# First batch of a fused attention and two-layer MoE kernel: softmax over rows of tokens straight from PSUM, wider key and value products, trees for phi, and a new order

## The chip, the cores and the metric

One core of one Trainium2 chip runs the kernel. The metric is the device time of one execution in microseconds (us), lower is better. Five engines work side by side: TensorE (PE, with its weight loads listed as PEld), VectorE (DVE), ScalarE (ACT), GpSimd (POOL), and SyncE (SP), which issues most DMAs.

## The reference, cut to what matters

Sizes: 4 batches, 8 heads, 576 tokens a batch, head dimension 64, 32 memory slots; model width 512, first hidden width 2048, then 4 experts of hidden width 1024. All is float32.

```
a    = softmax(phi, over the 32 slots)                  # per batch, head, token
k_m  = einsum('bhsm,bhsd->bhmd', a, k);  v_m = the same with v
attn = softmax(q @ k_m^T / 8, over the 32 slots)
x    = concat_heads(attn @ v_m)                         # 2304 x 512
h    = x @ w_in;  g = max(0.01 h, h);  x = g @ w_out    # first MoE layer
out  = sum over e of p_e * (relu(x @ w1[e]) @ w2[e])    # second layer
```

## The kernel before, in words

**The stages.** Attention of the four batches runs inside the first MoE layer; the second MoE layer follows. The first layer never forms `attn @ v_m`. For a chunk of 256 hidden features it multiplies `v_m` by `w_in` (`y_pair`, L984) and splits the result into a rounded high part and a low rest; the hidden product (`moe1_step`, L968) then multiplies that by the attention weights, which are split in the same way into `ah` and `al`: three products for each of two groups of heads, six matmuls of 128x288 for a half batch and a chunk of 128 features. ACT applies the leaky rectifier (L1023), ACT and DVE split again, and three times four matmuls (L1035 to L1037) multiply by a chunk of `w_out`. The first layer goes by units of features (6, 6 and 4 chunks of 128); in a unit come batch 0's first half of tokens with all chunks, its second half, then batch 1, and so on. So the first product of the layer needs batch 0's `ah` and `al` of the first half and the first `y`.

**One batch of attention** (`att_batch`, L540 to L741). 128 partitions hold 8 heads by 16 blocks, in 2 groups of 64 partitions. `phi` is loaded into `pl`, its maximum over 9 rows taken (`tree`, L552), finished over partitions by two PE transposes (L570, L576), subtracted (L578), and the exponential written to `a` (L581). For `k` and `v`, 72 products of a 64x32 piece of `a` with 64 columns accumulate over 9 rows (L617; each counts twice in the profile, as every float32 matmul here). The sum of `a` (L628, L633) gives the reciprocal `rz`, and ACT or DVE scales the products into `kv` (L641 to L655). Transposes give `kb` (L673 to L680) for the keys and `vt` for the values.

**Queries and scores before.** A batch in `TURNED` (batch 1 alone) transposes `q` with 20 PE transposes into `qT` (L586 to L601), copied out of PSUM by ACT; the others use one DVE transpose of 2304 elements in blocks of 32 (L603). Scores come out with the slots on partitions (L702), so for each half of the tokens DVE transposes them out of PSUM (L707, L713), takes the maximum (L720), subtracts (L722), ACT exponentiates (L725), DVE sums (L727), inverts (L729), multiplies (L733, or POOL), and transposes back (L736); `split` (L739) writes `ah` by ACT and `al` by DVE or POOL. Each half has its own such chain.

**Weights.** `w_in` and `w_out` are float64: `piece64` (L861) turns a 512 KB piece to float32 by two ACT passes (L877, L882), one of DVE (L888) and one of POOL (L887), and `w_out` is split as well. Raw pieces wait for three buffers and four places in `xx`.

**What sets the order.** `Plan` collects every operation with an engine, a cost, a due time and its dependences, and `issue` (L106) plays them as a list schedule in which the earliest due goes first. The order that comes out is each engine's program order, fixed before the run; the engines wait for each other by semaphores. `two=True` keeps a DVE operation from starting in the plan while POOL works, and the reverse. `SHIFTS` (L20) is a list of (first operation, count, us) added to due times by hand or search. `AFTER` (L748) says behind which step a later batch's loads enter the plan. `HOME` (L510) gives places: the queries of batches 0, 2 and 3 all lie in `A0`. While PE has nothing to do in the first 50 us the plan inserts idle matmuls (`idle`, L485).

## Time and profile before

| what | us |
|---|---|
| median of 3 runs (lowest, highest) | 1135.43 (1135.03, 1136.18) |
| the profiled execution, its own time | 1134.85 |
| its span, first to last instruction | 1133.0 |
| TensorE busy in the span | 1111.4 (98%) |
| first hidden product of the first layer (L968) starts | 33.11 |
| mean granted TensorE clock | 0.996 of full speed |

The span is counted from the first instruction; all times within the trace are from there. Between the span and the execution's own time lie 1.85 us that no instruction fills. In a row, "x" counts instructions, and a bracket at the end says how long the engine was idle before and what released it. A matmul's end is modelled, so consecutive matmuls overlap in the list; the distance between starts is what one costs.

### The profile page before, as it was taken

How to read it: one execution, taken by the hardware profiler on the slowest of the kernel's cores; microseconds unless marked ns; L12 is line 12 of the kernel's file. 1: busy time of each engine (PE TensorE's matmuls, PEld its weight loads, DVE VectorE, ACT ScalarE, POOL GpSimd, SP SyncE). 2: the span in 40 equal slices, each digit the busy share in tenths (PEclk: the TensorE clock that was granted, in tenths of full speed). 3: DMA queues.
4: the chain of work that ended last, by engine and by line, in shares of the span. 5: the costliest groups of instructions: out<-in, count | busy, mean ns of one | idle time of the engine just before them, and what ended most of it. 6: DMA issues, size and time to landing. Idle time of an engine off the chain costs nothing.

```text
span 1133.0 us, 18259 instructions
## 1 busy us (share of the span) xinstructions
PE 1111.4 (98%) x7478; PEld 1007.8 (89%) x7478; DVE 656.2 (58%) x1209; ACT 434.9 (38%) x889; POOL 98.9 (9%) x106
## 2 busy tenths in 40 slices
PE   4999999999999999999999999999999999999998
PEld 2788999999999998998998899889998889999887
DVE  6876645433437787677677653454576644454543
ACT  4854577633436444333334223222223223212220
POOL 3531035400000000000000000000000000000000
PEclk9999999999999999999999999999999999999999
DMA  9933024300002285554443744444344653344402
GB/s 358 313 113 120 2 76 132 113 1 2 20 1 103 87 317 192 204 205 188 156 165 133 223 161 156 167 167 157 130 139 168 171 212 138 127 154 167 168 19 56
DMA packets 54440, 160.86 MB, mean 142 GB/s; under 512 B 6484, under 2 KB 22868, under 8 KB 48212
## 3 DMA queue, kind: packets, MB, share of 16 engines
q1 hardware_dynamic: 49172, 100.19, 25.6%
q0 software_dynamic: 4608, 58.72, 14.7%
q8 instruction: 58, 0.95, 0.3%
q10 hardware_dynamic: 576, 0.79, 0.2%
q14 instruction: 26, 0.21, 0.1%
HBM read 125.60 MB, written 34.08 MB: 141 GB/s over the span
## 4 chain that ended last, share of the span: by engine, by line
PE 96%; DVE 1%; issue 1%; ACT 1%; DMA 0%; POOL 0%; POOLq 0%; DVEq 0%
PE psum L1144 31%; PE psum L1214 12%; PE psum L1213 12%; PE psum L1212 12%; PE psum L968 9%; PE psum L1035 6%; PE psum L1037 6%; PE psum L1036 6%; PE psum L984 2%; PE psum L617 1%; PE psum L702 1%; DVE exact L554 1%; DMA att<-in_phi_dram 0%; PE psum L487 0%; DVE att L603 0%
## 5 line engine op out<-in xcount | busy, mean ns | idle before, releaser
L1153 DVE TENSOR_TENSOR exact<-psum,exact 128x384 f32<-128x384 f32 x336 | 184.1, 556 | 271.8 <-PE psum L1144 267.8
L1160 ACT ACTIVATE rounded<-exact 128x384 fp32r<-128x384 f32 x192 | 100.9, 525 | 293.2 <-DVE exact L1153 291.4
L353 DVE TENSOR_TENSOR rounded<-exact,rounded 128x288 fp32r<-128x288 f32 (+3 forms) x221 | 120.6, 561 | 117.2 <-ACT rounded L350 116.5
L1214 PE MATMUL psum<-late,rounded 128*128 128x512 f32 x384 | 150.7, 392 | 0.0
L1213 PE MATMUL psum<-late,rounded 128*128 128x512 f32 x384 | 150.5, 392 | 0.0
L1212 PE MATMUL psum<-late,rounded 128*128 128x512 f32 x384 | 149.3, 389 | 0.0
L1144 PE MATMUL psum<-rounded 128*128 128x384 f32 x768 | 143.2, 335 | 0.0
L1144 PEld LDWEIGHTS psum<-rounded 128*128 128x128 f32 x768 | 134.7, 188 | 2.4 <-DVE exact L1153 0.3
L968 PE MATMUL psum<-rounded 128*128 128x288 f32 x768 | 122.6, 296 | 0.0
L350 ACT CAST rounded<-exact 128x288 fp32r<-128x288 f32 (+4 forms) x237 | 113.6, 500 | 14.6 <-DVE exact L836 4.4
L1035 PE MATMUL psum<-rounded 128*128 128x288 f32 x384 | 115.3, 300 | 0.0
L1036 PE MATMUL psum<-rounded 128*128 128x288 f32 x384 | 113.0, 294 | 0.7 <-DVE rounded L353 0.7
L1037 PE MATMUL psum<-rounded 128*128 128x288 f32 x384 | 112.9, 294 | 0.0
L968 PEld LDWEIGHTS psum<-rounded 128*128 128x128 f32 x768 | 108.1, 188 | 4.3 <-issue 3.9
L1144 PE MATMUL psum<-late,rounded 128*128 128x384 f32 x576 | 109.7, 336 | 0.0
L1164 DVE SCALAR_TENSOR_TENSOR rounded<-exact,rounded 128x384 fp32r<-128x384 f32 x192 | 98.9, 551 | 12.9 <-ACT rounded L1160 12.9
L1144 PEld LDWEIGHTS psum<-late,rounded 128*128 128x128 f32 x576 | 102.1, 188 | 3.8
L1175 ACT COPY exact<-psum 128x384 f32<-128x384 f32 x48 | 23.0, 480 | 196.8 <-PE psum L1144 196.8
L1023 ACT ACTIVATE exact<-psum 128x288 f32<-128x288 f32 x128 | 52.5, 410 | 119.9 <-PE psum L968 112.2
L1214 PEld LDWEIGHTS psum<-late,rounded 128*128 128x128 f32 x384 | 72.0, 188 | 15.1
L1213 PEld LDWEIGHTS psum<-late,rounded 128*128 128x128 f32 x384 | 72.0, 188 | 13.4
L1212 PEld LDWEIGHTS psum<-late,rounded 128*128 128x128 f32 x384 | 72.1, 188 | 13.2
(105 smaller groups left out, 1615.9 us busy)
## 6 DMA issues: line engine op xcount, KB each, us to landing
rounded<-kept POOLq DMA_DIRECT2D x22, 1792.0 KB, 7.7
exact<-in_moe_w_dram SPq DMA_DIRECT2D x64, 512.0 KB
kept<-rounded SPq DMA_DIRECT2D x10, 1792.0 KB
w<-kept POOLq DMA_DIRECT2D x10, 1792.0 KB, 7.8
kept<-w SPq DMA_DIRECT2D x6, 1792.0 KB
exact<-in_moe_w_in_dram SPq DMA_DIRECT2D x16, 512.0 KB
exact<-in_moe_w_out_dram SPq DMA_DIRECT2D x16, 512.0 KB
out_dram<-exact SPq DMA_DIRECT2D x60, 64.0 KB
```

Of the source, the lines that this page charges most:

```text
L350: nc.scalar.copy(out, in_) if e == "ACT" else engine(e).tensor_copy(out, in_)
L353: engine(e).tensor_tensor(out=out, in0=in0, in1=in1, op=ALU.subtract)
L968: nc.tensor.matmul(ps, lhsT=l, rhs=r, start=start and n == 0, stop=stop and n == len(seq) - 1)
L1035: nc.tensor.matmul(po, lhsT=w2l[:, ds_], rhs=th, start=first, stop=False)
L1036: nc.tensor.matmul(po, lhsT=w2h[:, ds_], rhs=tl, start=False, stop=False)
L1037: nc.tensor.matmul(po, lhsT=w2h[:, ds_], rhs=th, start=False, stop=last)
L1144: nc.tensor.matmul(ps[k][0:TB], lhsT=l, rhs=r, start=(i == 0), stop=(i == 5))
L1153: plan.op("DVE", dve2(TB), at[k], lambda: nc.vector.tensor_tensor(out=o, in0=ps[k][0:TB], in1=other, op=ALU.add), [ps[k], ok, from_], [key])
L1160: plan.op("ACT", act2(TB), at[k], lambda: nc.scalar.activation(out=th, in_=src, func=AF.Relu), [key, *h_from[hs[c, i]]], [keys[0]])
L1212: nc.tensor.matmul(po[0:DM], lhsT=tl, rhs=w2h[:, c], start=(p == 0 and c == 0), stop=False)
L1213: nc.tensor.matmul(po[0:DM], lhsT=th, rhs=w2l[:, c], start=False, stop=False)
L1214: nc.tensor.matmul(po[0:DM], lhsT=th, rhs=w2h[:, c], start=False, stop=(p == NP2 - 1 and c == 1))
```

## The change

For batch 0 alone: `phi`'s maximum and `a`'s sum become four DVE operations on halves (`tree`; for later batches also where DVE and not POOL takes it); the key and value products take two heads at a time, 64x64 pieces with 128 columns, of which the blocks off the diagonal are not used; the scaling by `rz` is four DVE operations for keys and four for values; `q` is transposed by PE (`TURNED` is now batch 0, so batch 1 goes the block way with L603). The scores come out with tokens on partitions, as 72 products of 64x64 by 32 columns in two parts (5 and 4 pairs of blocks of 64 tokens), so the softmax is done per part directly from PSUM, with no DVE transpose; the weights go to the place of `q`, 9 PE transposes turn them, and ACT and DVE write `ah` and `al` from PSUM, each part for both halves of the tokens. `q2` is loaded behind the `v` step together with `v1`. A number of costs and `two` flags change in the plan, and `SHIFTS` is a new list.

```
-SHIFTS = [(149, 1, 40.3), (286, 2, -1.2), (123, 1, 4.3), (232, 2, -1.2), (141, 8, 4.5), (4, 5, 25.2),
...
+SHIFTS = [(84, 27, 12.7), (94, 12, 5.9), (281, 8, 4.8), (683, 24, 24.5), (362, 33, 3.6), (85, 22, -17.5),
...
-    TURNED = (1,)
+    TURNED = (0,)
...
         def tree(fold, rows, e="DVE"):
-            if e == "DVE":
-                nc.vector.tensor_reduce(
-                    out=tops[:, 0:P].rearrange("p (h m) -> p h m", h=rows.shape[1]),
-                    in_=rows.rearrange("p h r m -> p h m r"), axis=AX.X, op=fold)
-                return
             h = rows.shape[1]
...
-            op("DVE", 1.35, due, lambda: tree(ALU.max, rows), ["pl"], ["aT1"])
+            op("DVE", 1.75, due, lambda: tree(ALU.max, rows), ["pl"], ["aT1"], two=True)
...
-                    for h in range(HG):
+                    for h in range(0, HG, 1 + wide):
                         for g in range(NGB):
...
+                            if wide:
+                                out_ = pkv[g * 512:g * 512 + 2 * D][h * M:(h + 2) * M].rearrange("p (h d) -> p h d", h=2)
+                                lhsT, rhs = a[gs, r, hs].rearrange("p h m -> p (h m)"), src[gs, 0, hs, r * D:(r + 1) * D]
...
+                    for h in range(HG):
+                        hs, at_d = slice(h * M, (h + 1) * M), h % 2 * D
+                        in_ = pkv[0:1024].rearrange("p (g n) -> p g n", g=NGB)[hs, :, at_d:at_d + D]
+                        nc.vector.tensor_tensor(out=kv[hs, :, lo], in0=in_, in1=rz[hs].unsqueeze(2).to_broadcast([M, NGB, D]),
+                                                op=ALU.mult)
+                op("DVE", 1.2, due, fn, [pkv, "rz0"], [f"kv{g}{nm}" for g in range(NGB) for nm in names])
...
+            for x in range(2):
+                rs, first, count = slice(x * D, (x + 1) * D), x * (LT + 1) // 2, (LT + 1 - x) // 2
+                n, groups = count * HG * M, slice(first * HG, (first + count) * HG)
...
+                    for j in range(count):
+                        for h in range(HG):
+                            for g in range(NGB):
+                                at_s = (j * HG + h) * M
+                                nc.tensor.matmul(
+                                    ps[at_s:at_s + M][g * D:(g + 1) * D], lhsT=qT[rs, j, h, g * D:(g + 1) * D],
+                                    rhs=kb[rs, g, h * M:(h + 1) * M], start=True, stop=True)
+                op("PE", 0.4 * count, due, fn, ["qT0", "qT1", "qT2", "kb"], [ps])
...
+                op("DVE", dve(n), due, lambda mx_=mx_, score=score: nc.vector.tensor_reduce(
+                    out=mx_, in_=score(), axis=AX.X, op=ALU.max), [ps], km)
+                op("DVE", dve(n), due, lambda mx_=mx_, raised=raised, full=full, score=score: nc.vector.tensor_tensor(
+                    out=raised[:, :, 0:M], in0=score(), in1=mx_.unsqueeze(2).to_broadcast(full), op=ALU.subtract),
...
+                op("ACT", act(n), due, lambda raised=raised: nc.scalar.activation(
+                    out=raised[:, :, 0:M], in_=raised[:, :, 0:M], func=AF.Exp, scale=scale), [], ka)
+                op("DVE", dve(n), due, lambda sm_=sm_, raised=raised: nc.vector.tensor_reduce(
+                    out=sm_, in_=raised, axis=AX.X, op=ALU.add), ka, ks)
+                op("DVE", 0.29, due, lambda sm_=sm_: nc.vector.reciprocal(sm_, sm_), [], ks)
+                op("DVE", dve(n), due, lambda e, sm_=sm_, raised=raised, full=full, weight=weight: engine(e).tensor_tensor(
...
+                   ka + ks, [f"e{x}"], room=[qn], also=("POOL", n * 2.03e-3), two=True)
+            for x, n, count, weight in parts:
+                pt = Banks(psum, 2 - x)
...
+                    for j in range(count):
+                        nc.tensor.transpose(pt[j * P:(j + 1) * P], weight[:, j * P:(j + 1) * P], ident)
+                op("PE", 0.12 * count + 0.1, due, fn, [f"e{x}", qn, "ident"], [pt])
+                for s in range(2):
...
+                    op("ACT", act(n // 2), due, lambda part=part, column=column: copy("ACT", part(ah), column()),
+                       [pt], [f"h{x}{s}"])
+                    op("DVE", dve(n // 2), due, lambda part=part, column=column: subtract(
+                        "DVE", part(al), column(), part(ah).bitcast(F32)), [pt, f"h{x}{s}"], [f"l{x}{s}"])
...
-        ("phi", 0): ["p1"], ("q", 0): ["q2"], ("v", 0): ["v1"],
+        ("phi", 0): ["p1"], ("v", 0): ["q2", "v1"],
```

In the chains of all later batches the subtraction (L722) and the multiplication (L733) get `two=True`, and the DVE shift in `piece64` (L888) is planned at 0.45 us where it was 0.42.

## Rows read from the trace of the kernel before

**Rows 1.** The page's head and busy lines: span, busy time and share of each engine.
```profile
span 1133.0 us, 18259 instructions
...
PE 1111.4 (98%) x7478; PEld 1007.8 (89%) x7478; DVE 656.2 (58%) x1209; ACT 434.9 (38%) x889; POOL 98.9 (9%) x106
```

**Rows 2.** TensorE by stretch: us, length, busy (count), granted clock, DMA share, GB/s.
```profile
33.10:40.00 6.90, 6.90 (x64) 1.00 0.93 331
40.00:45.00 5.00, 4.27 (x43) 1.00 0.88 334
45.00:50.00 5.00, 3.98 (x30) 1.00 0.74 220
50.00:100.00 50.00, 49.95 (x757) 1.00 0.52 170
```

**Rows 3.** Chain of waits, its longest pieces: start us, us, what.
```profile
4.91 2.09 DVE exact L554
...
22.00 3.67 issue
```

**Rows 4.** Engines by stretch: length; busy of PE, PEld, DVE, ACT, POOL; clock; DMA share, GB/s.
```profile
4.90:18.40 13.50, 7.97 (x172) 4.12 (x173) 10.99 (x12) 8.19 (x14) 3.97 (x3) 1.00 1.05 398
18.40:33.10 14.70, 9.62 (x248) 4.79 (x248) 11.34 (x16) 8.15 (x16) 6.35 (x5) 0.77 1.03 378
```

**Rows 5.** Timeline of the start, all engines: start us, us, engine, line, operation.
```profile
7.62 0.29 DVE L571 TENSOR_REDUCE att<-psum 128x2 f32<-128x128 f32 x1 [0.63 <-PE psum L570]
...
11.33 2.28 DVE L554 TENSOR_REDUCE exact<-att 128x128 f32<-128x1152 f32 x1 [1.23 <-ACT att L581]
...
11.84 1.67 PE L617 MATMUL psum<-exact,att 64*32 64x64 f32 x144
...
14.64 0.52 ACT L652 ACTIVATE exact<-psum,att 128x64 f32<-128x64 f32 x2 [0.46 <-DVE att L638]
...
15.68 2.56 DVE L603 STREAM_TRANSPOSE att<-att 128x2304 f32<-128x2304 f32 x1
...
18.18 0.38 DVE L888 TENSOR_SCALAR exact<-exact 128x512 uint32<-128x512 uint32 x1
...
18.39 1.98 PE L702 MATMUL psum<-att,exact 32*32 32x288 f32 x64 [1.49 <-DVE att L603]
...
23.10 0.68 ACT L725 ACTIVATE att<-att 128x576 f32<-128x576 f32 x1 [0.96 <-DVE att L722]
...
29.82 1.29 POOL L887 TENSOR_TENSOR w<-w,exact 128x512 uint32<-128x512 uint32 x1 [0.92 <-ACT exact L882]
29.88 1.85 DVE L722 TENSOR_TENSOR att<-att 128x576 f32<-128x576 f32 x1
...
31.66 0.68 DVE L353 TENSOR_TENSOR rounded<-psum,rounded 128x512 fp32r<-128x512 f32 x1
...
33.11 3.45 PE L968 MATMUL psum<-rounded 128*128 128x288 f32 x24
```

**Rows 6.** Timeline of TensorE, 39 to 70 us (batch 1).
```profile
42.68 1.51 PE L596 MATMUL psum<-att,exact 128*64 128x128 f32 x12
...
51.83 2.25 PE L617 MATMUL psum<-exact,att 64*32 64x128 f32 x144
...
56.81 0.67 PE L668 MATMUL psum<-att,exact 128*64 128x128 f32 x8
...
58.97 0.79 PE L702 MATMUL psum<-att,exact 64*32 64x160 f32 x32
```

**Rows 7.** Timeline of TensorE from 70 us (first hidden product of batch 1, then batch 2).
```profile
70.93 1.05 PE L968 MATMUL psum<-rounded 128*128 128x288 f32 x6
...
93.33 0.64 PE L673 MATMUL psum<-att,exact 128*32 128x128 f32 x16
...
95.27 1.24 PE L702 MATMUL psum<-att,exact 32*32 32x288 f32 x32
```

**Rows 8.** Timeline of VectorE, 59 to 82 us (batch 1's first y).
```profile
68.43 1.16 DVE L353 TENSOR_TENSOR rounded<-psum,rounded 128x1024 fp32r<-128x1024 f32 x1
```

More of the change, by code (lines that the diff above doesn't have):

```diff
@@ L499 @@
     qD = qT.rearrange("p a h n -> p (a h n)")[:, 0:HG * LT * D].rearrange("p (h c e t) -> p h c e t", h=HG, c=LT, e=2)
-    at = [tile_([NR, M + 1]) for i in range(2)]
+    both_at_ = tile_([2 * NR, M + 1])
+    at = [both_at_[:, i * NR:(i + 1) * NR] for i in range(2)]
     aT = [tile_([NGB, HB]), exact(NGB, HB)]
@@ L504 @@
     spare = exact(512)
-    small = {nm: [tile_([n]) for i in range(2)]
-             for nm, n in (("mx", NR), ("sm", NR), ("nmx", NGB), ("rz", NGB))}
+    small_ = {nm: tile_([2 * n]) for nm, n in (("mx", NR), ("sm", NR), ("nmx", NGB), ("rz", NGB))}
+    small = {nm: [t[:, 0:t.shape[1] // 2], t[:, t.shape[1] // 2:]] for nm, t in small_.items()}
     places = {"A": tile_([1, HG, S]), "X": xx.rearrange("p h (b s) -> p b h s", b=B)}
@@ L564, in att_batch @@
         if b == 0:
-            op("DVE", 1.35, due, lambda: tree(ALU.max, rows), ["pl"], ["aT1"])
+            op("DVE", 1.75, due, lambda: tree(ALU.max, rows), ["pl"], ["aT1"], two=True)
         else:
-            op("DVE", 1.35, due, lambda e: tree(ALU.max, rows, e), ["pl"], ["aT1"], also=("POOL", 3.0))
+            op("DVE", 1.75, due, lambda e: tree(ALU.max, rows, e), ["pl"], ["aT1"], also=("POOL", 3.0), two=True)
         mr = tops[:, 0:P]
@@ L628, in att_batch @@
                 if b == 0:
-                    op("DVE", 1.35, due, total, ["a"], ["aT1"])
+                    op("DVE", 1.75, due, total, ["a"], ["aT1"], two=True)
                 else:
-                    op("DVE", 1.35, due, lambda e, total=total: total(e=e), ["a"], ["aT1"], also=("POOL", 3.0))
+                    op("DVE", 1.75, due, lambda e, total=total: total(e=e), ["a"], ["aT1"], also=("POOL", 3.0), two=True)
                 pz = Banks(psum, 1)
@@ L640, in att_batch, with fn @@
             lo = "kv".index(sorted(names, key=lambda nm: HOME[nm][b])[0])
-            for g in range(NGB):
+            if b == 0:
+                def fn(pkv=pkv, lo=lo):
+                    for h in range(HG):
[4 more added lines that the diff above has]
+                op("DVE", 1.2, due, fn, [pkv, "rz0"], [f"kv{g}{nm}" for g in range(NGB) for nm in names])
+            for g in range(NGB if b else 0):
                 def fn(e, g=g, pkv=pkv, n=len(names), lo=lo):
@@ L723, in att_batch @@
                 out=at_r, in0=at_r, in1=mx.unsqueeze(2).to_broadcast(wide), op=ALU.subtract),
-               km, ka, also=("POOL", pool(S)))
+               km, ka, also=("POOL", pool(S)), two=True)
             op("ACT", act(S), due, lambda at_r=at_r: nc.scalar.activation(
@@ L734, in att_batch @@
                 out=at_r, in0=at_r, in1=sm.unsqueeze(2).to_broadcast(wide), op=ALU.mult),
-               ks, ka, also=eng[1])
+               ks, ka, also=eng[1], two=True)
             op("DVE", dve(S), due, lambda s=s, at_r=at_r: nc.vector.transpose(
@@ L887, in add @@
             engine(e).tensor_tensor(out=out, in0=fu, in1=low, op=ALU.add)
-        plan.op("DVE", 0.42, due, lambda: nc.vector.tensor_single_scalar(fu, fu, 3, op=ALU.logical_shift_left),
+        plan.op("DVE", 0.45, due, lambda: nc.vector.tensor_single_scalar(fu, fu, 3, op=ALU.logical_shift_left),
                 [], [fk], two=True)
```

40 lines of the change are left out of this document (31 added, 9 removed), and 10 rows, old and new, of the table SHIFTS.

## The prediction

> **What bounds the kernel now.** I read the page's head first: TensorE is busy 1111.4 of 1133.0 us [rows 1], so the end moves only if TensorE gets less to do, or starts its real work earlier, or loses less between. The stretches by engine show where it loses: from 50 us on it has no gap worth naming (49.95 of 50 us), while of the 16.9 us from 33.1 to 50 it is busy 6.90 + 4.27 + 3.98 = 15.15, so 1.75 us idle [rows 2]. Before 33.11 us no hidden product of the MoE layer runs; the first starts there [rows 5], and everything TensorE does earlier (batch 0's attention, the first `y`, idle matmuls) is in the shade of whoever makes that product wait. So the end is the start of that product, called S, plus the idle time behind S, plus TensorE's fixed work behind S. I write each part of the change as a shift of one of these three.
>
> Who sets S? In the chain of waits the start is phi's landing, a maximum of 2.09 us on VectorE and so on, and the stretch view has VectorE busy 10.99 of 13.5 us, then 11.34 of 14.7 us up to S; ACT stands at 8.19 and 8.15 [rows 3, 4]. Its idle time is hand-over time in a chain that is serial: product, maximum, subtraction, exponential, sum. VectorE is thus the engine to add up for S. The chain also has 3.67 us at 22.00 us in which TensorE waited for nothing that the profile shows ("issue") [rows 3], inside the value products, with the DMA share above 1 [rows 4].
>
> **The steps up to S.** The price of a VectorE pass comes from two rows: 0.29 us for 128 elements and 0.68 for 512, both out of PSUM [rows 5], so 1.02 ns an element more; 256 cost 0.42, 320 cost 0.49, 576 cost 0.75, 640 cost 0.81.
>
> *phi's trees.* Four operations of 512, 256, 128 and 128 elements: 0.68 + 0.42 + 0.29 + 0.29 = 1.68 us, in place of 2.09 [rows 3] and 2.28 [rows 5]. Both lie on the chain: the exponential ends 0.4 us earlier, at 10.9 (before, the sum started behind it at 11.33), the sum's tree at 12.6.
>
> *Key products.* Before, 144 instructions of 64 columns took 1.67 us; in batch 1 144 of 128 columns took 2.25 [rows 5, 6]. The change issues 72 of 128 columns. Half of 2.25 is the lower bound, 2.25 the upper one; I take 1.9, as the two rows show that most of the time is per instruction but 0.58 us came with the columns. They end near 13.4, beside the tree and the division that follows it, which ended 1.0 us behind the sum (13.61 to 14.64): so `rz` stands at 13.6 and sets the pace, and the products cost nothing; without that cover they cost at most 0.1.
> By the Trainium skill (TensorEngine Tiling (Array Packing), Available Configurations) pieces of 64x32 leave eight independent tiles and 64x64 only four, which speaks against the wide form; by it alone the products stay at 2.25 us, and S moves by under 0.1. No run yet shows the wide form.
>
> *Scaling and `kb`.* Four VectorE operations of 128 elements, 4 x 0.29 = 1.16 us, in place of 0.52 on ACT [rows 5]: 14.8. The turned form's transposes 0.67 [rows 6], a copy of about 0.4 (estimated between those passes): `kb` at 15.9.
>
> *Queries.* The 2.56 us transpose (15.68 to 18.24), for which the scores waited until 18.39 [rows 5], goes. In its place come 20 transposes on TensorE, 12 of which took 1.51 in batch 1 [rows 6], and three ACT copies of 1024, 1024 and 512 elements, about 1.1, 1.1 and 0.6 us at the exponential's 0.68 for 576 [rows 5]. `q` is there by 15.68 at the latest. Scores can then start between 16.0 (`kb` decides) and 18.4 (`q` lands just before 15.68); I take 16.8, nearer to `kb`.
>
> *Scores.* 72 products, 144 instructions of 32 columns in two parts of 80 and 64. Bounds: 11.6 ns each as in the key products (1.67 / 144) and 40 ns each as in the `kb` transposes of batch 2 (0.64 / 16) [rows 5, 7], so 0.9 to 3.2 us for part 0. The old scores had 31 ns (1.98 / 64), with 288 columns; I take 19 ns: 1.5 and 1.2 us. Part 0 is there at 18.3, part 1 hides behind its VectorE passes.
>
> *Softmax of both parts.* VectorE does maximum, subtraction, sum and multiplication over 640 and 512 elements, 4 x (0.81 + 0.68) = 6.0, and two inversions of some 0.3: 6.6 us, to 24.9. ACT's two exponentials (0.68 for 576 [rows 5]) each lie beside the other part's pass. Then, for the last part, transposes 0.5, ACT's copy 0.4, VectorE's subtraction 0.42: 26.2. No DVE transpose is left, but both halves of the tokens, not one, must be through before S.
>
> *What else VectorE must do by then.* The values' scaling 1.16, the rest of the first `y` 0.68, three integer shifts at 0.38 [rows 5]: 3.0 us. Little idle time is left to take them. So S = 26.2 + 3.0 + 0.2 for hand-overs = 29.4, a gain of 3.7. If all of it fits into gaps, S is 26.4 (gain 6.7). If scores start at 18.4 and TensorE's 3.67 us stop falls onto the path, S is 34.7 (loss 1.6).
>
> **Behind S.** *Batch 1 loses the turned form.* TensorE's work there: 20 transposes at 1.51 / 12 = 2.5, then 0.67, then two scores of 0.79 = 4.8 us [rows 6]; in the block form, as in batch 2, 0.64 + 2 x 1.24 = 3.1 [rows 7]. The durations overlap at their ends, so I count 1.2 of the 1.7 us: gain 1.2 (0.9 to 1.7). VectorE pays 2.56 more for the block transpose and saves about 0.6 on the score transposes.
>
> *Idle time behind S.* The first unit's weights are converted at the pace of ACT, POOL and the DMA (share still 0.93 and 0.88 [rows 2]), and nothing in the change speeds them. A start 3.7 us earlier meets them earlier: 0 to 3.7 back. But the half-1 softmax that VectorE did for batch 0 behind S is gone, which is what some of the 1.75 us waited behind. I take 1.0 back.
>
> *Batch 1's due point.* Its first hidden product ran at 70.93, and the `y` it needs was written at 68.43 + 1.16 = 69.6 [rows 7, 8]. In the forecast TensorE arrives at 70.93 - 3.7 - 1.2 + 1.0 = 67.0. VectorE was freed of some 3 us for batch 0 before that, and does 2.0 more for batch 1; I take 0.5 us of waiting.
>
> *At no cost:* `q2` and `v1` share one entry point now. SP's queue takes them in program order; `q2` goes to the place where batch 0's weights now lie, so its load waits for their transposes (about 25) rather than for the old `q` transpose (18.24), and holds whatever stands behind it on SP. The cover is that batch 1's key and value products ran only at 51.83 [rows 6]; without it that is a wait of up to 7 us for those loads. Other costs in the plan only move the order.
>
> **Sum.** -3.7 - 1.2 + 1.0 + 0.5 = -3.4 us on the profiled execution's 1134.85 us (span 1133.0 plus 1.85): 1131.45. That execution is 0.6 below the median of the three runs; I forecast 1131.5.
>
> **Rivals.**
> 1. *The weights decide.* TensorE starts early and then waits for `w_out` pieces; the DMA share near 1 up to 40 us [rows 2, 4] speaks for it, that TensorE was fully busy from 33.1 to 40 [rows 2] against it. All 3.7 come back, 1.2 stays: 1133.7 to 1135. Or TensorE's stop of 3.67 us lands among the scores, with the same result. Chance 0.21.
> 2. *The short start.* VectorE's other work finds gaps, S is 26.4, and no more than 1.0 comes back: -6.7 - 1.2 + 1.0 = -6.9, about 1128. For it: VectorE had 3.4 us idle between 18.4 and 33.1 [rows 4]. Against it: the longer chain uses them. Chance 0.19.
> 3. *Slower: VectorE is late with batch 1.* While POOL ran at 29.82 for 1.29 us, the subtraction of 576 elements issued at 29.88 took 1.85 instead of 0.75 us [rows 5]: it stood until POOL was done. Trees, subtractions and multiplications, the operations with two SBUF inputs, are six groups in batch 1, four of them new or newly held back in the plan; each can lose up to 1.1. With 2.0 for the block transpose that is 6.4 us, and if two thirds of it come, `y` and tokens are ready at 69.6 + 4.3 = 73.9 and TensorE stands still until then: end +3.0, about 1138. It decides from the point where batch 1 is ready later than 70.93. Chance 0.13.
> The Trainium skill (SBUF — State Buffer, section "SBUF: two separate sides") says that VectorE, in an operation with two SBUF inputs, and GpSimd exclude each other for the whole instruction; the 1.85 us agree. By it a tree can lose what a reduction over one input would not, which is this rival.
>
> **How the numbers follow.** The forecast, -2.3 to -5.5, has 0.47. Faster by over 0.2% (2.3 us, about what a measurement of this kernel can tell from no change) holds the forecast and rival 2: 0.66. Within 0.2% is rival 1: 0.21. Slower is rival 3: 0.13. The range leaves out the far ends of rivals 2 and 3: 1126.5 (S at 26.4 with nothing given back and 1.7 for batch 1 would be 1126.4) to 1136.5.
>
> **What would show it.** Right: the first L968 near 29.4; trees of about 1.7 us; no L603 and no L707 before it, PSUM passes of 0.81 and 0.68; 20 transposes at 43 us gone; idle TensorE between S and 50 us of 2 to 3 us. Wrong: an S above 33; TensorE idle more than 5 us between S and 75; a wait before batch 1's first hidden product; the first hidden products at a lower granted clock than before.

## The result: slower by 11.2 us, and the profile after

| what | before | after |
|---|---|---|
| median (lowest, highest; runs), us | 1135.28 (1135.03, 1136.18; 4) | 1146.49 (1145.03, 1148.37; 4) |
| span of the profiled execution, us | 1133.0 | 1143.3 |
| first hidden product, us | 33.11 | 34.87 |
| TensorE idle from there to 60 us, us | 1.80 | 8.45 |

The ratio is 1.0098 (95% interval 1.0078 to 1.0118). The forecast was 1131.5 us (1126.5 to 1136.5), a gain; the change lost time instead. "Before" in the table has one run more than the kernel before was shown with.

The page's head of the changed kernel, against [rows 1]:

```profile
span 1143.3 us, 18155 instructions
...
PE 1124.3 (98%) x7429; PEld 1016.5 (89%) x7429; DVE 660.9 (58%) x1243; ACT 431.8 (38%) x885; POOL 95.4 (8%) x102
```

TensorE is still busy 98%, but its busy time grew by 12.9 us though it has 49 instructions less; 11.5 of the 12.9 lie ahead of the first hidden product (29.08 against 17.60 us). A busy TensorE at half clock and one that runs idle matmuls look the same in this line; the stretches tell them apart, against [rows 2, 4] (us, length, busy (count) of PE, PEld, DVE, ACT and POOL, granted clock, DMA share, GB/s):

```profile
25.00:30.00 5.00, 5.00 (x51) 2.88 (x50) 3.33 (x6) 3.21 (x7) 0.00 (x0) 0.50 1.06 391
...
34.87:50.00 15.13, 11.11 (x87) 9.53 (x86) 13.85 (x18) 7.49 (x17) 9.01 (x8) 1.00 0.89 319
50.00:60.00 10.00, 5.57 (x157) 4.83 (x158) 5.71 (x11) 3.94 (x10) 3.49 (x3) 0.83 0.84 271
60.00:100.00 40.00, 40.00 (x518) 34.85 (x524) 25.00 (x45) 22.85 (x53) 8.81 (x7) 1.00 0.40 127
```

From 60 us on TensorE is idle 4.74 us where it was 4.31, so almost all of the loss lies in front: from 34.87 to 60 us TensorE is idle 4.02 + 4.43 = 8.45 us, and from 25 to 30 us it is busy all the time at a granted clock of 0.50, the lower level (1.2 GHz).

The timeline of TensorE behind the first hidden product (start us, us, engine, line, operation; in brackets the idle time before it and what released it):

```profile
34.87 0.40 PE L1032 MATMUL psum<-rounded 128*128 128x288 f32 x1
35.93 3.29 PE L1032 MATMUL psum<-rounded 128*128 128x288 f32 x23 [0.66 <-DVE rounded L349]
41.69 0.30 PE L562 MATMUL psum<-att,exact 128*128 128x128 f32 x1 [2.48 <-DVE exact L555]
41.83 1.02 PE L483 MATMUL psum<-att 128*128 128x512 f32 x2
...
52.54 0.38 PE L625 MATMUL psum<-att,exact 128*128 128x2 f32 x2 [3.42 <-DMA exact<-in_v_dram]
53.14 3.40 PE L615 MATMUL psum<-exact,att 64*32 64x128 f32 x136 [0.22 <-DVE att L629]
58.21 0.42 PE L615 MATMUL psum<-exact,att 64*32 64x128 f32 x8 [1.67 <-issue]
```

Three waits make up 7.6 of the 8.45 us: 2.48 for batch 1's maximum (L555), 3.42 ahead of its sum (L625), and a stop of 1.67 within its key and value products. These products took 3.40 + 0.42 us where [rows 6] had 2.25: the granted clock, 0.83 as a mean of 50 to 60 us, was 0.50 from 54 to 57, behind TensorE's longest wait. In the kernel before, the wait for the maximum was 0.78 us, and the key and value products (51.83 [rows 6]) stood ahead of the sum's product and covered it:

```profile
45.77 0.30 PE L570 MATMUL psum<-att,exact 128*128 128x128 f32 x1 [0.78 <-DVE exact L554]
...
54.01 0.38 PE L633 MATMUL psum<-att,exact 128*128 128x2 f32 x2
```

In the new order the sum's product stands ahead of them. No run moved that alone.

What VectorE did in front of the first two waits (its timeline, same columns):

```profile
36.73 1.78 DVE L555 TENSOR_TENSOR exact<-att 128x512 f32<-128x512 f32 x1
38.54 2.68 DVE L555 TENSOR_TENSOR exact<-exact 128x256 f32<-128x256 f32 x2
41.26 0.29 DVE L555 TENSOR_TENSOR exact<-exact,att 128x128 f32<-128x128 f32 x1
...
45.86 1.55 DVE L952 TENSOR_SCALAR exact<-exact 128x512 uint32<-128x512 uint32 x1
47.33 2.57 DVE L595 STREAM_TRANSPOSE att<-exact 128x2304 f32<-128x2304 f32 x1
49.83 1.55 DVE L555 TENSOR_TENSOR exact<-att 128x512 f32<-128x512 f32 x1
51.41 0.75 DVE L555 TENSOR_TENSOR exact<-exact 128x256 f32<-128x256 f32 x2
52.20 0.29 DVE L555 TENSOR_TENSOR exact<-exact,att 128x128 f32<-128x128 f32 x1
```

The tree of the maximum lasts 36.73 to 41.55, 4.8 us in place of 1.7. The block transpose of batch 1's queries, which the kernel before did not have, stands ahead of the tree of the sum, for which TensorE waits; the sum's product starts 0.05 us behind that tree's end (52.49). The shift in front of it (L952), an operation with one input that the prediction did not count among those that lose, took 1.55 us beside a GpSimd instruction (45.66, 1.47 us) in place of 0.42. In the kernel before VectorE had time to spare there:

```profile
50.55 2.34 DVE L554 TENSOR_REDUCE exact<-att 128x128 f32<-128x1152 f32 x1 [1.24 <-ACT att L581]
```

The wait of 3.42 us names a DMA of `v` as the releaser; the chain of waits (start us, us, what) runs through VectorE instead:

```profile
45.95 1.47 DVE exact L952
47.41 2.49 DVE att L595
49.90 1.49 DVE exact L555
```

Sum: start +1.76, idle time behind it +6.65, batch 1's products +1.57, idle matmuls behind the start +1.02, batch 1 un-turned -1.2 as forecast: 9.8 of the 10.3 us by which the span grew. The idle time behind 60 us adds 0.43. TensorE's busy time behind the start grew by 1.47 us (1095.24 against 1093.77), which leaves -1.1 for the un-turned batch beside the two other busy terms.

Ahead of the first hidden product, the timeline of GpSimd and VectorE in batch 0's sum:

```profile
10.69 1.28 POOL L951 TENSOR_TENSOR exact<-exact 128x512 uint32<-128x512 uint32 x1 [8.95 <-DVE exact L948]
10.89 1.62 DVE L555 TENSOR_TENSOR exact<-att 128x512 f32<-128x512 f32 x1 [0.35 <-ACT att L573]
...
12.55 1.71 DVE L555 TENSOR_TENSOR exact<-exact 128x256 f32<-128x256 f32 x2
12.70 1.42 POOL L349 TENSOR_TENSOR rounded<-exact,rounded 128x512 fp32r<-128x512 f32 x1 [0.73 <-ACT rounded L346]
14.29 0.29 DVE L555 TENSOR_TENSOR exact<-exact,att 128x128 f32<-128x128 f32 x1
```

and TensorE from the key products to the scores of batch 0:

```profile
11.62 2.83 PE L615 MATMUL psum<-exact,att 64*64 64x128 f32 x72
14.37 1.09 PE L588 MATMUL psum<-att 128*128 128x128 f32 x8
15.30 0.28 PE L625 MATMUL psum<-att,exact 128*128 128x2 f32 x2
...
19.77 1.31 PE L705 MATMUL psum<-exact,att 64*64 64x32 f32 x40
21.38 1.35 PE L705 MATMUL psum<-exact,att 64*64 64x32 f32 x40 [0.30 <-issue]
...
23.03 3.52 PE L705 MATMUL psum<-exact,att 64*64 64x32 f32 x64
```

The tree's first row starts while a GpSimd instruction runs and ends 0.54 us behind it (12.51 against 11.97); its second row ends 0.14 us behind the next one (14.26 against 14.12). The tree takes 3.7 us and ends at 14.58. The sum's product stands in TensorE's order behind eight query transposes, and runs only at 15.30: TensorE was busy without a gap from 8.06 to 21.08 us, where the kernel before was idle 2.90 of the 12.50 us from 8.50 to 21.00. The first row of the scores takes 33 ns an instruction at a granted clock of 1.00, part 1 takes 55 at 0.52.

### The profile page after: what moved, and what is told of

The parts are those of the page before. It is cut to its first block, busy times and chain, and to the rows that moved or that the text cites. A ratio compares the mean times of both kernels' runs of the same rounds, so it can differ in the third digit from the quotient of the medians.

```text
span 1143.3 us, 18155 instructions
## 1 busy us (share of the span) xinstructions
PE 1124.3 (98%) x7429; PEld 1016.5 (89%) x7429; DVE 660.9 (58%) x1243; ACT 431.8 (38%) x885; POOL 95.4 (8%) x102
## 4 chain that ended last, share of the span: by engine, by line
PE 96%; DVE 1%; DMA 1%; issue 0%; POOL 0%; SPq 0%; ACT 0%; DVEq 0%; POOLq 0%
PE psum L1208 31%; PE psum L1278 12%; PE psum L1277 12%; PE psum L1276 11%; PE psum L1032 9%; PE psum L1099 6%; PE psum L1100 6%; PE psum L1101 6%; PE psum L1048 1%; PE psum L615 1%; PE psum L766 1%; DMA exact<-in_k_dram 1%; PE psum L705 1%; DVE exact L555 0%; DMA att<-in_phi_dram 0%
## 5 line engine op out<-in xcount | busy, mean ns | idle before, releaser
L346 ACT CAST rounded<-exact 128x288 fp32r<-128x288 f32 (+2 forms) x238 | 113.8, 499 | 13.4 <-DVE exact L900 3.8
L1228 DVE SCALAR_TENSOR_TENSOR rounded<-exact,rounded 128x384 fp32r<-128x384 f32 x192 | 98.8, 550 | 12.9 <-ACT rounded L1224 12.9
```

What stands on the lines that cost most here:

```text
L346: nc.scalar.copy(out, in_) if e == "ACT" else engine(e).tensor_copy(out, in_)
```

## The experiments

The theory from these rows: VectorE's order and its stretched trees hold batch 1 up (rival 3 of the prediction, but at batch 1's maximum and sum). Rivals: the loads of `q2`, `q1`, `k1` on SP's queue; the slow score products before the start; the form of batch 0's softmax itself. Every engine's order is that of the kernel that the run is made from, except for an operation that a diff moves, and except in the runs with another list of shifts or other turned batches, where the plan is made anew. Where an operation is moved, `issue` records the list of operations first, changes it and plays it. Differences are of medians, against the changed kernel's 1146.49 us where its edits are meant. Medians of the kernel before, taken beside the runs, were 1135.01 us (first four runs), 1135.02 (next four), 1135.14 (next four) and 1134.58 (last four). Each trace is of one execution.

**Reductions instead of trees** (changed kernel):

```
         def tree(fold, rows, e="DVE"):
+            if e == "DVE":
+                nc.vector.tensor_reduce(
+                    out=tops[:, 0:P].rearrange("p (h m) -> p h m", h=rows.shape[1]),
+                    in_=rows.rearrange("p h r m -> p h m r"), axis=AX.X, op=fold)
+                return
```

> The changed kernel with phi's maximum and a's sum as one VectorE reduction each again, every engine's order of work as in the changed kernel. Tree theory (trees stretched by GpSimd make VectorE late, 3.7 us for the sum of batch 0 and 4.8 us for the maximum of batch 1): the time falls by 3 to 6 us, to about 1141 us. Score theory (batch 0's scores are slow and hold VectorE's queue): falls by 1 to 2 us only, since the wait for the scores stays. Queue theory (q2's load holds SP): no change, within 1 us.

1144.11 us (ratio 1.0076, 1.0059 to 1.0093): -2.4, between the two theories' ranges, with intervals that overlap and two profiled spans that are alike (1143.6 and 1143.3). Batch 1's maximum took 2.32 us in place of 4.8, and the wait of 2.48 us for it went (0.79 us for a split came near its place); the wait before the sum stayed, at 2.89, and behind it the key and value products took 4.7 us at a clock of 0.50. Batch 0's sum was there at 13.39, 1.2 us earlier, but its product still ran at 15.22 and the first hidden product at 35.05: the tree of batch 0's sum did not set the start.

**`q2` behind `k1` on SP** (changed kernel; one DMA moved):

```
+    def later(calls):
+        n, m = [[i for i, c in enumerate(calls) if c[0] == loaded[name]][0] for name in ("q2", "k1")]
...
+        return calls[:n] + calls[n + 1:m + 1] + [calls[n]] + calls[m + 1:]
-    plan.issue()
+    plan.issue(later)
```

> The changed kernel with one DMA moved: q2's load is issued behind k1's instead of ahead of q1's and k1's; all other orders as in the changed kernel. Queue theory: the DMA gap between 31 and 36 us closes, k1 lands 3 us or more earlier, the time falls by 3 to 7 us. Tree and score theories: the loads behind q2 wait for pieces of weights that GpSimd has not converted yet, so they start at most 1 us earlier and the time moves by less than 1 us.

1148.37 us (1.0116, 1.0101 to 1.0131). `q1` was issued at 31.16 instead of 34.66, and the waits stayed at 2.47 and 3.42 us. `q2`'s place decides nothing here. `k1` came only 0.4 us earlier (36.74 against 37.11), so its own load was hardly tested; that the wait before the sum fell with every load left in its place (block transpose, below) is the better evidence against the loads.

**A quarter of the score products** (changed kernel): 18 products of 128 columns in place of 72 of 32, from the first head's queries alone, so the queries of three heads out of four are left out.

```
-                        for h in range(HG):
-                            for g in range(NGB):
-                                at_s = (j * HG + h) * M
-                                nc.tensor.matmul(
-                                    ps[at_s:at_s + M][g * D:(g + 1) * D], lhsT=qT[rs, j, h, g * D:(g + 1) * D],
-                                    rhs=kb[rs, g, h * M:(h + 1) * M], start=True, stop=True)
+                        for g in range(NGB):
+                            at_s = j * HG * M
+                            nc.tensor.matmul(
+                                ps[at_s:at_s + HG * M][g * D:(g + 1) * D], lhsT=qT[rs, j, 0, g * D:(g + 1) * D],
+                                rhs=kb[rs, g, 0:HG * M], start=True, stop=True)
```

> The changed kernel with batch 0's scores as 18 products of 128 columns from the queries of head 0 for all four heads, where the change has 72 products of 32 columns (what is left out: the queries of heads 1 to 3 in each group). Same columns, a quarter of the instructions and weight loads. Score theory: the two parts take about 0.7 us each instead of 3.0 and 3.5, part 1's maximum comes 4 us earlier, and the time falls by 4 to 8 us. Tree theory: 1 to 2 us. Queue theory: 1 to 3 us, as q2 is released earlier.

1143.72 us (1.0075, 1.006 to 1.009): -2.8, less than the 4 to 8 us of the theory that the scores are all of it. Its timeline of TensorE and one of its stretches (PE alone):

```profile
21.39 1.09 PE L704 MATMUL psum<-exact,att 64*64 64x128 f32 x16
```
```profile
25.00:30.00 5.00, 3.20 (x21) 1.00 1.06 391
```

Part 1 took 1.09 us in place of 3.52, the clock stayed at 1.00 although TensorE was *less* busy, and the first hidden product came at 32.75, 2.1 earlier. The waits behind it stayed the same size (2.47 and 3.42): nothing of the earlier start was given back.

**Narrow key products** (changed kernel): batch 0's key and value products as before, with the scaling that belongs to them.

```
-            def fn(rs_, pkv=pkv, src=src, n=len(names), wide=b == 0):
+            def fn(rs_, pkv=pkv, src=src, n=len(names), wide=False):
...
-                    for h in range(HG):
-                        hs, at_d = slice(h * M, (h + 1) * M), h % 2 * D
-                        in_ = pkv[0:1024].rearrange("p (g n) -> p g n", g=NGB)[hs, :, at_d:at_d + D]
-                        nc.vector.tensor_tensor(out=kv[hs, :, lo], in0=in_, in1=rz[hs].unsqueeze(2).to_broadcast([M, NGB, D]),
-                                                op=ALU.mult)
+                    for g in range(NGB):
+                        nc.vector.tensor_scalar_mul(kv[:, g, lo], pkv[g * 512:g * 512 + D], rz[:, g:g + 1])
```

> The changed kernel with batch 0's key and value products one head at a time again (64x32 pieces by 64 columns) and the scaling as two VectorE operations each, order as in the changed kernel. If the wide form costs what its rows say (2.8 us for the keys against 1.67 before), and the keys' scaling 1.19 against some 0.4, kb comes 1 to 2 us earlier and the time falls by 1 to 3 us. If the sum of a on VectorE sets the pace there, as I forecast, it falls by less than 1 us.

1151.08 us (1.0141, 1.0126 to 1.0156): +4.6, not less, with the first hidden product at 39.93. Its timeline of TensorE shows TensorE standing for nothing that the profile shows:

```profile
18.12 0.69 PE L615 MATMUL psum<-exact,att 64*32 64x64 f32 x44 [1.52 <-issue]
24.32 2.88 PE L702 MATMUL psum<-exact,att 64*64 64x32 f32 x50 [2.88 <-issue]
```

The first stands within the narrow value products, the second among the scores (L702), whose form was not changed. The 3.67 us stop of the kernel before [rows 3] is of this kind and lies within narrow products. The changed kernel's own stop ahead of the start is 0.30 us, a gain that the prediction did not count. What the stop is was not settled, and its size changes from trace to trace: among the same scores behind wide products it was 0.30 to 0.82 us or none in the kernels with a list of shifts, 1.39 us without one.

**The block transpose behind the sum** (changed kernel; one VectorE operation moved, 75 behind 79, the sum's division):

```
+    def behind(calls):
+        n, m = [[i for i, c in enumerate(calls) if c[0] == k][0] for k in (75, 79)]
...
+        return calls[:n] + calls[n + 1:m + 1] + [calls[n]] + calls[m + 1:]
-    plan.issue()
+    plan.issue(behind)
```

> The changed kernel with one VectorE instruction moved: batch 1's block transpose of q (2.57 us) stands behind batch 1's sum and division instead of in front of them; all other orders as in the changed kernel. Theory now: behind S TensorE waits for batch 1's chain on VectorE, which the block form made longer; the wait of 3.42 us ahead of batch 1's key and value products falls to about 1 us and those products keep the full clock, so the time falls by 2 to 5 us. Rival (it is the trees that hold VectorE, or the late loads of q1 and k1): less than 1 us.

1142.62 us (1.0066, 1.0046 to 1.0085): -3.9 for the place of one instruction, each run below each run of the changed kernel. VectorE's timeline:

```profile
47.63 0.68 DVE L557 TENSOR_TENSOR exact<-att 128x512 f32<-128x512 f32 x1
48.34 1.74 DVE L557 TENSOR_TENSOR exact<-exact 128x256 f32<-128x256 f32 x2
50.11 0.29 DVE L557 TENSOR_TENSOR exact<-exact,att 128x128 f32<-128x128 f32 x1
...
51.89 2.58 DVE L597 STREAM_TRANSPOSE att<-exact 128x2304 f32<-128x2304 f32 x1
```

The sum is there at 50.40 in place of 52.49, the wait of 3.42 us shrank to 0.55 and 0.69, and the granted clock of 50 to 60 us went from 0.83 to 1.00. The fall of the clock did not vanish, it came earlier: 0.62 from 42 to 46 us, behind the wait of 2.46 us for the maximum, where the changed kernel had 1.00.

**Both: block transpose behind, reductions.**

> The two edits together: block transpose of batch 1 behind the sum, and one-instruction reductions in place of the trees. If the two waits (2.47 us for the maximum, 3.42 us for the sum) are one after the other on the same chain, both go and the time falls by 5 to 8 us, to about 1140 us. If the end is set by weights that come late instead, it falls by no more than the larger of the two edits alone (2 to 3 us).

1139.08 us (1.0033, 1.0023 to 1.0044): -7.4 of the 11.2 us, the two alone together (2.4 + 3.9) within the spread. With the block transpose moved, the reductions are worth 3.5 us, clear of the spread. TensorE's idle time from the first hidden product (34.41) to 60 us is 25.59 - 21.83 = 3.76 us, and the clock stays at 1.00 all that time.

**The lists of shifts left empty**, in the changed kernel and in the one before:

```
-SHIFTS = [
...
+SHIFTS = [
 ]
```

> The changed kernel with an empty list of shifts: the order is what due times alone give. If the new form itself costs the time, this kernel is as far from the kernel before with an empty list (next run) as the two are with their lists, 9 to 13 us. If the list of shifts is what is worse, the two without lists lie within 4 us.

> The kernel before with an empty list of shifts. Its list is worth 5 to 10 us if the order around the start is what was tuned: about 1140 to 1145 us. See the run ahead of it for what the distance of the two tells.

1148.16 us (1.0112, 1.0074 to 1.015) for the change, 1147.54 us (1.0106, 1.0082 to 1.0131) for the kernel before, two runs each. Without a list the two medians lie within 1 us of each other, the change's two runs 5.6 us apart (1145.36 and 1150.97). The old list is worth 12.5 us to the old kernel, more than expected; the new list 1.7 us, less than the spread, to the new one. This points to an order that suits the new form less well, but it does not show it: the two lose in different places. In the traces without a list the change starts its first hidden product at 38.93 and the kernel before at 33.49, while TensorE's idle time from there to 100 us is 4.92 against 8.04 us.

**Trees in the kernel before**, all four batches:

```
         def tree(fold, rows, e="DVE"):
-            if e == "DVE":
-                nc.vector.tensor_reduce(
-                    out=tops[:, 0:P].rearrange("p (h m) -> p h m", h=rows.shape[1]),
-                    in_=rows.rearrange("p h r m -> p h m r"), axis=AX.X, op=fold)
-                return
```

> The kernel before, every engine's order kept, with phi's maximum and the sum of its exponentials as four VectorE operations on halves instead of one reduction (four batches; later batches only where VectorE and not GpSimd takes it). Trees stretched by GpSimd (the theory): 1.7 us each where GpSimd is idle, up to 4 us where it runs; batch 0's maximum gains 0.4 us, its sum and batch 1's pair lose 1 to 2 us each; the first hidden product 0.5 to 1.5 us later than 33.1, and the time 1136 to 1138 us. Trees as cheap as their passes (the prediction): first product 0.5 us earlier, 1134.5 us.

1137.23 us (1.0014, 1.0005 to 1.0023): +1.6 by the ratio. VectorE's timeline in batch 1's maximum, and TensorE's wait for it:

```profile
42.14 1.78 DVE L558 TENSOR_TENSOR exact<-att 128x512 f32<-128x512 f32 x1 [0.33 <-POOL rounded L353]
43.96 0.75 DVE L558 TENSOR_TENSOR exact<-exact 128x256 f32<-128x256 f32 x2
44.75 1.39 DVE L558 TENSOR_TENSOR exact<-exact,att 128x128 f32<-128x128 f32 x1
```
```profile
46.28 0.30 PE L565 MATMUL psum<-att,exact 128*128 128x128 f32 x1 [2.54 <-DVE exact L558]
```

4.0 us where the reduction had 2.25; the wait grew from 0.78 to 2.54 us. In batch 0, with GpSimd idle, the same four operations took 1.8 us, and the first hidden product came at 32.07, 1.0 earlier, where the theory had it later. Not all of that is the tree: the value products came 0.36 us earlier (20.28 against 20.64), and the stop of 3.67 us within them was 2.76. The tree alone is harmless in one batch and bad in the next.

**The kernel before without turned queries** (batch 1 by the block transpose; list renumbered, less two entries for operations that are gone, plan made anew):

```
-    TURNED = (1,)
+    TURNED = ()
```

> The kernel before with batch 1's queries by VectorE's block transpose (2.56 us) instead of 20 TensorE transposes, nothing else of the change; the list of shifts is the one of before, renumbered, and the plan is made anew with it. TensorE has 1.2 us less to do. If only TensorE's work counts (the prediction): 1134 us. If VectorE's time ahead of batch 1's key and value products counts (the theory): the block transpose lands in front of the sum or of the first score transposes, idle time of 1 to 3 us appears between 45 and 75 us, and the time is 1135 to 1138 us.

1141.47 us (1.0055, 1.0043 to 1.0068): +6.3, more than either theory gave. The block transpose (42.48, 2.57 us) stands ahead of batch 1's maximum (46.37); TensorE waits 1.74 us there, then 2.16 us for a GpSimd split at 59.49, and is idle 4.63 us up to 60 where the kernel before had 1.80. Here also the order was made anew, so the run shows the part together with its order.

**The changed kernel with both batches turned:**

```
-    TURNED = (0,)
+    TURNED = (0, 1)
```

> The changed kernel with batch 1's queries turned on TensorE too, as in the kernel before (list of shifts renumbered, the plan made anew with it): VectorE loses the block transpose of 2.57 us that stands before batch 1's sum, TensorE has 1.2 to 1.7 us more. Theory: the wait of 3.4 us before batch 1's keys and values shrinks to under 1 us and the time is 1143 to 1145 us (the changed kernel less 3 to 4 us as with the transpose moved behind, plus 1.2 to 1.7 us of TensorE's work). If that wait has another cause (a load, the weights): it stays above 2.5 us, and the time is 1147 to 1149 us.

1148.73 us (1.012, 1.0105 to 1.0134). The wait before the sum fell to 1.45 us, between the theory's "under 1" and the other side's "above 2.5", and the new order brought 1.10 us for GpSimd and an issue stop of 3.33 us within batch 1's products. The time met the other side's number. With the plan made anew, a theory about one wait does not predict the time.

**Three costs off**: block transpose behind, reductions, a quarter of the score products (the same queries left out).

> The changed kernel with batch 1's block transpose behind its sum, reductions instead of trees, and batch 0's score products as 18 of 128 columns from the first head's queries (the queries of the other three heads of a group are left out). The run with the first two edits alone gave 1139.1 us with the first hidden product at 34.4. If the score products' slow issue at half clock is the rest of the late start: first product at 32.3 to 32.8, time 1136.5 to 1137.5 us. If an earlier start is given back behind it (as in the run with this edit alone, where 2.1 us of start gave 2.8 of time, it was not): start 32.5 but time 1139 us.

1137.81 us (1.0022, 1.0013 to 1.0031): 1.3 less than the two edits without it, with intervals that overlap, and first hidden product at 32.91, both just beyond the ranges expected. That start is 0.2 ahead of the kernel before, with 4.38 us idle up to 100 us in place of 1.80.

**Without the last two idle matmuls** (changed kernel; the plan's filling at 34.00 and 41.83 us):

```
+    def unfilled(calls):
+        fills = [i for i, c in enumerate(calls) if c[0] is None]
+        return [c for i, c in enumerate(calls) if i not in fills[-2:]]
-    plan.issue()
+    plan.issue(unfilled)
```

> The changed kernel without the last two idle matmuls that the plan inserts (they ran at 34.00 and 41.83 us, 1.02 us each; the kernel before has none behind its first hidden product). If they cost their length: the one at 34.00 stands straight ahead of the first hidden product and the one at 41.83 straight behind a wait, so 0.9 to 1.9 us less, 1144.6 to 1145.6 us. If they fill time in which TensorE would wait anyway: no difference, or slower should the clock fall: 1146.5 us or more.

1147.99 us (1.011, 1.0093 to 1.0127; single runs from 1143.3 to 1149.7), no different from the changed kernel by the intervals. The profiled one, the fastest, began its first hidden product at 33.31, and then the clock fell, to a mean of 0.66 from 35 to 40 us:

```profile
34.39 4.83 PE L1034 MATMUL psum<-rounded 128*128 128x288 f32 x23 [0.68 <-DVE rounded L351]
```

The same 23 products that took 3.29 us took 4.83 here. That is one execution, and leaving the filling out is not enough for it: the two runs with three edits, below, leave out the same idle matmuls, and there these products took 3.30 us at a clock of 1.00. Leaving the filling out gained nothing; what lowered the clock is open.

**Three edits that compute everything**: block transpose behind, reductions, no late idle matmuls.

> The changed kernel with batch 1's block transpose behind its sum, reductions for trees, and without the last two idle matmuls. The first two edits gave 1139.1 us. If the idle matmuls cost their length: 1137.2 to 1138.2 us. If they only fill: 1139 us.

1140.39 us (1.0048, 1.0036 to 1.0061): nothing gained over the two edits. TensorE is idle 4.30 us in place of 3.76, so half of what had been filled became idle time. The 1.02 us in the sum above is in that part a wait with another name.

**Trees in batch 0 alone, in the kernel before:** `if e == "DVE" and b > 0:` ahead of the reduction.

> The kernel before, its order kept, with trees for the maximum and sum of batch 0 alone. In the run with trees everywhere the first hidden product came at 32.07 instead of 33.11 us and the wait for batch 1's maximum was 2.54 instead of 0.78 us. If trees cost only where GpSimd runs beside them: first product at 32.1, batch 1 as before, so 1134.0 to 1134.5 us, faster than both kernels. If the earlier start is given back at the weights: 1135 us.

1135.28 us (1.0003, 0.9994 to 1.0012): no difference. Its waits in batch 1 are those of before (0.80 for the maximum), so the loss with trees everywhere came from the later batches. The gain at the start did not come; in the profiled execution the first hidden product ran at 34.59, with a granted clock of 0.50 and 0.56 from 25 to 35 us. There the stop within the value products was 4.74 us, against 3.67 in the kernel before and 2.76 with trees everywhere, whose start was the earliest of the three. The start follows that stop, which no edit aimed at, through all three.

**The three edits with batch 0's maximum as a tree:**

> As the changed kernel with the three edits (block transpose behind the sum, reductions, no late idle matmuls), but batch 0's maximum stays a tree, where GpSimd is idle. A tree there took 1.75 us and a reduction 2.1: 0.3 us less than the run without it. If the step that decides the start does not go through phi's maximum: the same within 0.2 us.

1139.33 us (1.0036, 1.0022 to 1.005), 1.1 below the run without it, with intervals that overlap. No version tried beats the kernel before.

## Why the prediction was wrong, step by step

*The frame held.* Start, idle time behind it and TensorE's fixed work carry the result (9.8 of 10.3, and 0.4 of idle time behind 60 us). Two of its terms failed, by about as much: the start (-3.7 forecast, +1.76 measured) and the idle time behind it (1.0 and 0.5 forecast, +6.65 measured).

*The start*, forecast 29.4, came at 34.87. The step that failed is "VectorE is thus the engine to add up for S". Up to the scores TensorE's order set the pace, and the scores themselves were priced too low.
- The maximum's tree: 1.68 forecast, 4.82 to 6.62 measured, right. The sum's tree: 1.68 forecast, 3.7 measured. The prediction priced it by PSUM passes and kept the GpSimd rows [rows 5] for a rival. It was covered, though: with a reduction the sum was there 1.2 us earlier and the start was the same.
- Key products: 1.9 forecast with 2.25 as the upper bound, 2.83 measured (72 instructions, 39 ns each). The same 72 took from 2.19 to 3.20 us in the other traces of this form, at a clock of 1.00; what spreads them was not found. By the Trainium skill's rule on tiles (TensorEngine Tiling (Array Packing), Available Configurations) the prediction had them stay at 2.25. The traces lie on both sides of that and do not decide it.
- `rz` was expected at 13.6, behind the sum on VectorE, with the products at no cost. It came at 16.0, because the sum's product stood behind the key products and eight query transposes; the products of `kb` stood behind value products in the same way (17.92, the scaling having ended at 17.21), and `kb` came at 19.0 (15.9). The scaling was right (1.19 against 1.16). The scores so began at 19.77, 3.0 later than taken and beyond the bound of 18.4.
- Scores: 1.5 and 1.2 us forecast, 3.0 and 3.5 measured. Part 1 hid behind nothing: the maximum over it waited 2.13 us. The 55 ns at half clock lie above the upper bound of 40. With a quarter of the products the start came 2.1 us earlier. The Trainium skill (TensorE: Matmul & The Clock Gate, "Wait — 56ns, not 53.3ns?") gives some 25 ns as the least from start to start of two small matmuls. The 33 ns at the higher level lie above that and the 19 ns taken lay below it. The narrow key products [rows 5] ran 11.6 ns apart, though, so here the figure is no floor for every form.
- The VectorE passes over PSUM were right (0.69 and 0.68 for 512).

*The idle time behind the start* is the other step that failed: "I take 1.0 back" became 6.65. The reason given, that batch 0's second half no longer waits there, looked at what leaves VectorE and not at what comes. The block transpose was counted (2.56 us) but placed at batch 1's first hidden product at 70.93, where 0.5 us of waiting was allowed. It stands instead, by the new order, in front of batch 1's sum at 47 us, where TensorE had nothing else to run in its order. The runs with its place changed (-3.9) and with reductions as well (-7.4) show this.

*The clock behind a wait* was in no term. After 3.42 us of waiting the key and value products of batch 1 took 3.82 us in place of 2.25. In the six traces of the changed kernel's order with 1.9 to 3.4 us of waiting there they took 3.5 to 4.7 us, in the five with two waits of at most 0.8 us 2.25 to 2.6.

*Batch 1 un-turned*: TensorE's 1.2 us came (the busy times above leave 1.1), but the run of that part alone in the kernel before, with its order made anew, was 6.3 us slower. A saving on the engine that bounds the kernel was bought with a longer operation in front of a serial chain.

*`q2` on SP at no cost*: right as far as tested. `q2` waited 6.9 us and held `q1` and `k1`, and issuing `q1` 3.5 us earlier changed nothing.

*The rivals.* Rival 3 had the mechanism (VectorE late with batch 1 through stretched trees and the block transpose) and the sign. Its point of decision, 70.93, was 20 us too late, so its price of +3.0 was too small. Rival 1's stop among the scores was 0.30 us, and none of the three waits behind the start was for a weight. Rival 2 needed a start at 26.4.

*Still open:* why three costs off remain 2.7 us behind the kernel before. Its span is 3.3 us longer: -0.2 for the start, +2.6 idle up to 100 us, +0.4 idle behind that and +0.6 of TensorE's busy time. The idle time is spread over waits of 0.2 to 1.2 us, and none of them was taken apart. Whether the new list could be made as good for the new form as the old one is for the old was not tried, nor was the place of the sum's products in TensorE's order.

## What to carry to other kernels

When an operation moves to another engine, ask first what will stand behind it in that engine's program order, and who waits for that; its length is the smaller question. One block transpose moved behind a sum was worth 3.9 us, as much as the whole gain forecast. Before adding up the engine that looks busiest, check that no other engine's order stands in front of the steps: here TensorE, without a gap, held the sum's product. A tree of two-input VectorE operations is shorter than a reduction only while GpSimd is idle: 1.8 us there, 2.7 to 4.8 beside it, against 2.1 to 2.3; and even there it gained no time. A hand-tuned order belongs to the form it was tuned on, so compare two forms with both lists off as well, and look where each then loses.

## What was not expected of the hardware

- TensorE's clock fell to 0.50 while the profile showed it busy all through 25 to 30 us, with products of 64x64 by 32 columns before and idle matmuls behind. All eleven traces with these 72 products had stretches at 0.50 between 23 and 35 us; the two with a quarter of them stayed at 1.00, though busy only 3.20 and 3.06 of 5 us. These products are not needed for a fall: the kernel before also had 0.52 from 25 to 30 us, behind its stop of 3.67 us. Busy time alone does not tell the clock.
- TensorE stops of up to 4.74 us in which it waits for nothing that the profile shows stand in the first 70 us of most traces, and the same program part had 2.76, 3.67 and 4.74 us of them in three kernels that differ ahead of it only in VectorE's reductions.
- The tree of the sum beside GpSimd took 3.7 us in place of 1.8; operations that started beside a GpSimd instruction ended 0.54 and 0.14 us behind its end. That agrees with the exclusive lock of the Trainium skill (SBUF — State Buffer, "SBUF: two separate sides").
